# Geglu's x @ w_gate as four 32-row tiles of TensorE side by side, with x and the weights laid out by token block, and the output projection moved to the end

## The chip, the cores and the metric

The kernel runs on one core of a Trainium2 chip. The metric is device time in microseconds (us) of one execution; smaller is better. The profile of an execution is taken by the hardware profiler. Its engines are called PE (TensorE: matrix products), PEld (TensorE's weight loads, which are instructions of their own), DVE (VectorE), ACT (ScalarE), POOL (GpSimd) and SP (SyncE, which here issues every DMA, in the order of its queue). Matrix products write to PSUM, which has eight banks of 512 float32 columns; DVE and ACT read the results from there.

## The reference, cut to what matters

The output is a gated mix of an attention block and a geglu block over the same x (2048 tokens of width 448). The hidden width F is 1792, and there are 16 heads of 28.

```python
def _A_ref(x, wqkv, wo):            # attention, H = 16, Dh = 28
    q, k, v = split(x @ wqkv)
    p = softmax(q @ k.T * Dh ** -0.5)
    return merge_heads(p @ v) @ wo  # the output projection

def _B_ref(x, w_gate, w_up, w_down):
    return (_gelu(x @ w_gate) * (x @ w_up)) @ w_down

g = _sigmoid((x * gate_w).sum(-1, keepdims=True))
return g * _A_ref(x, wqkv, wo) + (1 - g) * _B_ref(x, w_gate, w_up, w_down)
```

Everything is float32. The kernel takes a float32 product as three products of a faster format (float32r): each operand is split exactly into hi + lo, and hi·hi + lo·hi + hi·lo is summed.

## The kernel before, in words

There are three stages. In the first, q, k, v and the gate's logits are made (tiles `pqk`, `pv`). In the second, attention runs head by head: score tiles `sc`, exp on ACT into `pt`, and values `po`, which are four products of 32 output columns each that stand side by side on TensorE. While ACT works on exp, TensorE takes `x @ w_up` in between, one product after the other, for all 14 tiles of 128 hidden columns (`pu`); it also takes `x @ w_gate` for the hidden tiles 0, 1 and 2 (NB = 3). The results (`u`) go to DRAM (`ud`) and are read back in the third stage.

The third stage is geglu, and the change is there. The hidden width is worked through in 7 chunks of FC = 2 tiles f of 128 columns, in the order (2, 3, 1, 4, 0, 5, 6), so it begins with the tiles 4 and 5. The tokens come in NTB = 4 blocks tb of 512. For each chunk and each block, `hidden(f, tb)` makes the gate product `pg`: 11 products of 128 rows of the contraction by 128 hidden columns by 512 tokens (the 448 rows are three tiles of 128 and one of 64, whose hi and lo parts share a tile; this is the list PAIRS). It needs no new x, since X with its hi and lo parts has been in SBUF since the first stage. For f < 3 `pg` is read from DRAM instead (`gs`). Then ACT applies gelu (L389), DVE multiplies by u (L390), ACT copies the hi part (L391) and DVE subtracts for the lo part (L392): the tile `hl2`. After a chunk's block, `down` takes the product with w_down for the block before it: 4 token tiles of 128, 6 products of 448 columns each into `pd`, and DVE adds each into `acc` (L407, L409). `load_f` fetches the weights of the next hidden tile in time: `load_half` (one DMA of 256 KB, hi on ACT L236, lo on DVE L232) and w_down (`draw`, `w`).

The output projection of attention is done in the middle of that stage: `load_wo` in chunk number 1, and in the chunks 2 and 3 `load_o` and `project` for each token block, 44 products of 448 columns that DVE adds into `acc` too. The last chunk's `down` adds `acc` into `y` and writes it out (L412, L413).

Matrix products keep the program's order (`mm`, L47). All other instructions are ordered by a scheduler when the kernel is built, so the order on SP, ACT and DVE is not quite that of the source. A tile that is allocated again waits until the readers of the older tile in its buffer are done; `bufs` says how many buffers a name has. The softmax division of a head (`finish`, L273 to L290) goes through DRAM in four steps on SP's queue: `dend`, `r`, `rdend`, `rb`, and then the result `od`; each step waits for the one before it.

Of the kernel before, what the change touches and what calls it, by code (L numbers as in the profile page):

```python
# [11 lines left out]
OP = mybir.AluOpType  # L12
# [30 lines left out]
def gated_mix(ctx: ExitStack, tc: tile.TileContext, xT, wqk, wvg, wg, wu, wd, wo, sel, ident, out):  # L43
# [18 lines left out]
    vp = attn.enter_context(tc.tile_pool(name="vp", bufs=1))  # L62
# [8 lines left out]
    with ExitStack() as ph:  # L71
# [74 lines left out]
        # |q.k| <= (sum of q's squared maxima + sum of k's) / 2, by head  # L146
# [28 lines left out]
        # g = 1 / (1 + exp(-t))  # L175
# [47 lines left out]
    gp = ctx.enter_context(tc.tile_pool(name="gp", bufs=1, side="right"))  # L223
# [15 lines left out]
    with ExitStack() as ph:  # L239
# [52 lines left out]
        def up():  # L292
            # x @ w_up, a product at a time
# [63 lines left out]
    with ExitStack() as ph:  # L357
        ap = ph.enter_context(tc.tile_pool(name="ap", bufs=1, reuse_waits="tile"))
        acc = ap.tile([P, NT, D], F32, name="acc")
        hp = ph.enter_context(tc.tile_pool(name="hp", bufs=2, reuse_waits="tile"))  # L360
        tp = ph.enter_context(tc.tile_pool(name="tp", bufs=3, reuse_waits="tile"))
        wpo = ph.enter_context(tc.tile_pool(name="wpo", bufs=1, reuse_waits="tile"))
        psg = ph.enter_context(tc.tile_pool(name="psg", bufs=3, space=PSUM, reuse_waits="tile"))
        psd = ph.enter_context(tc.tile_pool(name="psd", bufs=5, space=PSUM, reuse_waits="tile"))
        WD = {}

        def load_f(f):
# [3 lines left out]
            w = gp.tile([P, 2, D], F32R, name="w", bufs=3)  # L371
# [5 lines left out]
        def hidden(f, tb, hl):  # L377
            s = slice(tb * TB, (tb + 1) * TB)
            u = tp.tile([P, TB], F32, name="u")
            nc.sync.dma_start(out=u, in_=ud[f, :, s])  # L380
            g = tp.tile([P, TB], F32, name="g")
            if f < NB:
                pg = tp.tile([P, TB], F32, name="gs")
                nc.sync.dma_start(out=pg, in_=ud[NF + f, :, s])
            else:
                pg = psg.tile([P, TB], F32, name="pg")
                for i, (x, w) in enumerate(PAIRS):
                    mm(pg, halves["g", f][:, w], X[:, x, s], i == 0, i == len(PAIRS) - 1)
# [63 lines left out]
        for n in range(NF // FC):  # L452
            for tb in range(NTB):
                hls = []
                for k in range(n * FC, (n + 1) * FC):
                    if tb == 0 and k + 1 < NF:
                        load_f(order[k + 1])
# [48 lines left out]
```

## Time and profile before

| | |
|---|---|
| time, median of 2 runs | 1068.47 us (1068.43 to 1068.51) |
| span of the profiled execution (first to last instruction) | 1068.0 us |
| PE busy | 1054.2 us (99%), 5664 matrix products |
| ACT, DVE, POOL busy | 616.8, 320.2 and 41.5 us |
| geglu stage on PE | 777.5 to 1063.7 us of the span |
| DMA | 115.85 MB, 108 GB/s over the span |

In the page's groups, a row gives the line, the engine, the operation, out<-in by the program's names, the shapes (for PE rows contraction*output columns comes first) and the count; then the busy time of the group, the mean duration of one in ns, and the idle time of the engine just ahead of them with what ended it. Matrix products overlap in the pipeline, so that a group's busy time divided by its count, not the mean duration, says how long one keeps PE. Busy times, chains and timelines are in us from the start of the span.

### The profile page before, as it was taken

To read this page: it belongs to the slowest core of one execution; us is meant where nothing else is said; L and a number is where in the kernel's file an instruction comes from. 1 tells how busy PE (TensorE), PEld (TensorE's weight loads), DVE (VectorE), ACT (ScalarE), POOL (GpSimd) and SP (SyncE) were. 2 spreads that over 40 slices of the span, in tenths; PEclk is the share of its full clock that TensorE was granted. 3 is DMA by queue.
4 is the path that set the end of the run, shared out by engine and by line. 5 is a ranking of instruction groups with operands and counts; after the bars stand their busy time and mean duration, and the time that the engine had idled before them with its cause. 6 is when DMAs were issued, how large, how long until landed. Compare 5 with 4: busy or idle time off the path is not lost.

```text
span 1068.0 us, 14546 instructions
## 1 busy us (share of the span) xinstructions
PE 1054.2 (99%) x5664; PEld 732.2 (69%) x5664; DVE 320.2 (30%) x519; ACT 616.8 (58%) x732; POOL 41.5 (4%) x32
## 2 busy tenths in 40 slices
PE   7999999999999999999999999999999999999998
PEld 5789756556556556556556566565588888888887
DVE  5561111111111111110110110110156656577555
ACT  6322478778777777777777787787643332233321
POOL 5300000000000000000000000000001011100000
PEclk9999999999999999999999999999999999999999
DMA  8875122332332332342332332331164323342233
GB/s 267 291 258 145 57 75 73 120 103 73 102 103 74 98 107 73 94 112 73 94 112 73 93 111 73 94 102 41 64 191 142 99 86 91 95 148 67 63 87 115
DMA packets 58907, 115.85 MB, mean 108 GB/s; under 512 B 12784, under 2 KB 18160, under 8 KB 55216
## 3 DMA queue, kind: packets, MB, share of 16 engines
q1 hardware_dynamic: 58832, 114.85, 35.8%
q8 instruction: 47, 0.77, 0.3%
q14 instruction: 28, 0.23, 0.1%
HBM read 74.44 MB, written 40.37 MB: 108 GB/s over the span
## 4 chain that ended last, share of the span: by engine, by line
PE 88%; DVE 0%; issue 0%; DVEq 0%
PE sc L47 23%; PE po L47 21%; PE pd L47 16%; PE pu L47 16%; PE pg L47 11%; DVE u L307 0%; DVE y L412 0%; DVE gate L178 0%; DVE gate L177 0%; DVE gate L179 0%; DVEq L307 0%
## 5 line engine op out<-in xcount | busy, mean ns | idle before, releaser
L261 ACT ACTIVATE pt<-sc 128x1024 f32<-128x1024 f32 x512 | 482.4, 1026 | 164.6 <-PE sc L47 163.9
L47 PE MATMUL sc<-Q,K 114*128 114x512 f32 x1024 | 317.9, 402 | 1.3 <-issue 1.3
L47 PEld LDWEIGHTS sc<-Q,K 114*128 114x128 f32 x1024 | 188.8, 189 | 94.3 <-issue 54.5
L47 PE MATMUL pu<-X,half 128*128 128x512 f32 x748 | 237.8, 397 | 0.4 <-DVE u L307 0.3
L47 PE MATMUL po<-pt,V 128*32 128x512 f32 x2048 | 233.0, 595 | 0.0
L307 DVE COPY u<-pu 128x512 f32<-128x512 f32 x68 | 47.0, 691 | 491.6 <-PE pu L47 484.7
L47 PEld LDWEIGHTS pu<-X,half 128*128 128x128 f32 x748 | 141.0, 189 | 35.9 <-issue 1.4
L47 PEld LDWEIGHTS po<-pt,V 128*32 128x32 f32 x2048 | 60.0, 109 | 137.8 <-issue 132.2
L47 PE MATMUL pd<-w,hl 128*128 128x448 f32 x672 | 140.9, 366 | 0.0
L47 PEld LDWEIGHTS pd<-w,hl 128*128 128x128 f32 x672 | 126.2, 188 | 12.2
L47 PE MATMUL pg<-X,half 128*128 128x512 f32 x484 | 116.6, 395 | 0.0
L47 PEld LDWEIGHTS pg<-X,half 128*128 128x128 f32 x484 | 90.7, 187 | 20.9
L47 PE MATMUL pqk<-X,WQK 128*128 128x512 f32 x308 | 75.0, 404 | 7.7 <-ACT X L104 6.0
L47 PEld LDWEIGHTS pqk<-X,WQK 128*128 128x128 f32 x308 | 58.6, 192 | 23.7 <-ACT X L104 6.9
L389 ACT ACTIVATE g<-pg 128x512 f32<-128x512 f32 x44 | 26.2, 595 | 78.7 <-PE pg L47 78.6
L390 DVE TENSOR_TENSOR g<-g,u 128x512 f32<-128x512 f32 x56 | 46.0, 830 | 55.0 <-ACT g L389 55.0
L391 ACT ACTIVATE hl<-g 128x512 fp32r<-128x512 f32 x56 | 35.2, 630 | 42.4 <-DVE g L390 36.6
L409 DVE SCALAR_TENSOR_TENSOR acc<-pd,gate,acc 128x448 f32<-128x448 f32 x80 | 53.0, 679 | 6.8 <-PE pd L47 6.8
L437 POOL TENSOR_TENSOR ohl<-oraw,ohl 128x1536 fp32r<-128x1536 f32 x4 | 14.0, 3511 | 752.0 <-DMA u<-ud 749.2
L392 DVE TENSOR_TENSOR hl<-g,hl 128x512 fp32r<-128x512 f32 x56 | 38.3, 687 | 10.6 <-ACT hl L391 8.7
L47 PE MATMUL pd<-WO,ohl 128*128 128x448 f32 x176 | 37.0, 368 | 0.0
L47 PE MATMUL pv<-WV,X 128*128 128x450 f32 x176 | 36.4, 366 | 0.0
(60 smaller groups left out, 325.1 us busy)
## 6 DMA issues: line engine op xcount, KB each, us to landing
ud<-u SPq DMA_DIRECT2D x68, 256.0 KB
qkd<-hl SPq DMA_DIRECT2D x28, 512.0 KB
Q<-qkd SPq DMA_DIRECT2D x64, 224.0 KB
K<-qkd SPq DMA_DIRECT2D x64, 224.0 KB
u<-ud SPq DMA_DIRECT2D x56, 256.0 KB
raw<-in_xT SPq DMA_DIRECT2D x16, 256.0 KB
rb<-rdend SPq DMA_DIRECT2D x64, 64.0 KB
hraw<-in_wu SPq DMA_DIRECT2D x14, 256.0 KB
```

The source lines that it names most:

```text
L47: tc.keep_in_program_order(nc.tensor.matmul(o, lhsT, rhs, start=start, stop=stop))
L261: nc.scalar.activation(pt, sc, AF.Exp, scale=SCALE)
L307: nc.vector.tensor_copy(u, p)
L389: nc.scalar.activation(g, pg, AF.Gelu_apprx_tanh)
L390: nc.vector.tensor_tensor(g, g, u, OP.mult)
L391: nc.scalar.activation(hl[:, 0], g, AF.Copy)
L392: nc.vector.tensor_tensor(hl[:, 1], g, hl[:, 0].bitcast(F32), OP.subtract)
L409: nc.vector.scalar_tensor_tensor(acc[:, t], p, g1, acc[:, t], OP.mult, OP.add)
L437: nc.gpsimd.tensor_tensor(O[:, 4:7], o[:, 0:3], O[:, 0:3].bitcast(F32), OP.subtract)
```

## The change: what it does

The four token blocks of one hidden tile are now worked on together, each on 32 rows of TensorE. The contraction of 448 rows is cut into NCH = 14 chunks of 32. The new tile X2 holds x so that token block tb lies on the partitions 32·tb to 32·tb + 31 for all 14 chunks, as hi and lo. The weights `w2` of a hidden tile hold the same 14 chunks, copied onto all four groups of 32 partitions. For each chunk and each of the three hi/lo pairs, four products of 32 rows by 128 hidden columns by 512 tokens follow each other, one for each token block, into four PSUM banks: 14 × 3 × 4 = 168 products for a hidden tile, where there were 44.

With it come these changes:

- X and the pool `fw` are given up at the end of attention, and X2 is made from DRAM at the start of geglu (`load_x2`): 7 rounds, each with 8 DMAs of 64 KB into the one buffer `x2r`, a copy on ACT (hi) and a subtraction on DVE (lo).
- The weights of a hidden tile come by 16 DMAs into the one buffer `w2r`, in place of one DMA; the copy and the subtraction are 128x1792 in place of 128x512.
- The order of the chunks is (0, 1, ..., 6), so that geglu begins with the hidden tiles 0, 1 and 2, whose gate products come from DRAM.
- `hidden(f)` does all four blocks; two `down` of the chunk before follow each `hidden`. `psg` has 4 PSUM banks (3 before), `psd` 4 (5 before), `hl2` 10 buffers (4 before), `w` 5 (3 before), `u` 4 and `gs` 2 (3 before).
- The output projection with its loads comes last, after the last `down`; it adds `acc` into `y` and writes out. X2's memory is given up for it.

```diff
-ORDER = (2, 3, 1, 4, 0, 5, 6)   # chunks of the hidden width
+ORDER = (0, 1, 2, 3, 4, 5, 6)
+NCH = D // 32
...
-    X = keep.tile([P, 7, S], F32R, name="X")
-    fw = ctx.enter_context(tc.tile_pool(name="fw", bufs=2))
     attn = ctx.enter_context(ExitStack())
+    X = attn.enter_context(tc.tile_pool(name="xp", bufs=1)).tile([P, 7, S], F32R, name="X")
+    fw = attn.enter_context(tc.tile_pool(name="fw", bufs=2))
...
-        psg = ph.enter_context(tc.tile_pool(name="psg", bufs=3, space=PSUM, reuse_waits="tile"))
-        psd = ph.enter_context(tc.tile_pool(name="psd", bufs=5, space=PSUM, reuse_waits="tile"))
+        psg = ph.enter_context(tc.tile_pool(name="psg", bufs=4, space=PSUM, reuse_waits="tile"))
+        psd = ph.enter_context(tc.tile_pool(name="psd", bufs=4, space=PSUM, reuse_waits="tile"))
...
+        X2 = x2p.tile([P, 2, NCH, TB], F32R, name="X2")
+        def chunks(dst, src, q, g):
+            n = 4 if q < 2 else 3
+            nc.sync.dma_start(out=dst[32 * g:32 * g + 32, q:q + 4 * (n - 1) + 1:4], in_=src[32 * q:32 * q + 32, 0:n])
+        def load_x2():
+            for b in range(0, NCH, 2):
+                x2r = x2p.tile([P, 2, TB], F32, name="x2r", bufs=1)
+                for tb in range(NTB):
+                    for i in range(2):
+                        c = b + i
+                        nc.sync.dma_start(out=x2r[32 * tb:32 * tb + 32, i], in_=xT[tb, 32 * (c % 4):32 * (c % 4) + 32, c // 4])
+                nc.scalar.activation(X2[:, 0, b:b + 2], x2r, AF.Copy)
+                nc.vector.tensor_tensor(X2[:, 1, b:b + 2], x2r, X2[:, 0, b:b + 2].bitcast(F32), OP.subtract)
...
         def load_f(f):
             if f >= NB:
-                load_half(wg, f, "g", by_act)
+                w2r = w2p.tile([P, NCH, P], F32, name="w2r", bufs=1)
+                for q in range(4):
+                    for g in range(4):
+                        chunks(w2r, wg[f], q, g)
+                w2 = w2p.tile([P, 2, NCH, P], F32R, name="w2")
+                nc.scalar.activation(w2[:, 0], w2r, AF.Copy)
+                nc.vector.tensor_tensor(w2[:, 1], w2r, w2[:, 0].bitcast(F32), OP.subtract)
...
-                for i, (x, w) in enumerate(PAIRS):
-                    mm(pg, halves["g", f][:, w], X[:, x, s], i == 0, i == len(PAIRS) - 1)
+                steps = [(c, x, w) for c in range(NCH) for x, w in ((0, 0), (1, 0), (0, 1))]
+                for k, (c, x, w) in enumerate(steps):
+                    for tb in range(NTB):
+                        r = slice(32 * tb, 32 * tb + 32)
+                        mm(pgs[tb], WG2[f][r, w, c], X2[r, x, c], k == 0, k == len(steps) - 1)
...
+                made.append(hidden(order[k]))
+                for _ in range(2):
+                    if pend:
+                        down(*pend.pop(0))
+            pend = [(n, tb, [m[tb] for m in made]) for tb in range(NTB)]
+        xs.close()
...
+        load_wo()
+        for tb in range(NTB):
+            load_o(tb)
+        for p in pend:
+            down(*p)
+        for tb in range(NTB):
+            project(tb)
```

The order on PE where attention ends and geglu begins, before (names with numbers; `po` and `pu` are attention's last products, `pg` gate products, `pd` products with w_down):

```order
L47 MATMUL po_7755<-pt_7952,V_74 32x512 x2
L47 MATMUL pu_8005<-X_66,half_7610 128x512 x11
L47 MATMUL pg_8071<-X_66,half_8048 128x512 x11
L47 MATMUL pg_8101<-X_66,half_8058 128x512 x11
L47 MATMUL pg_8121<-X_66,half_8048 128x512 x11
L47 MATMUL pg_8141<-X_66,half_8058 128x512 x11
L47 MATMUL pd_8157<-w_8053,hl2_8067 128x448 x3
```

The same place on PE in the changed kernel:

```order
L48 MATMUL po_7755<-pt_7952,V_77 32x512 x2
L48 MATMUL pu_8005<-X_70,half_7610 128x512 x11
L48 MATMUL pd_8292<-w_8133,hl2_8159 128x448 x3
L48 MATMUL pd_8292<-w_8138,hl2_8204 128x448 x3
L48 MATMUL pd_8300<-w_8133,hl2_8159 128x448 x3
L48 MATMUL pd_8300<-w_8138,hl2_8204 128x448 x3
```

Ahead, four gate products of 11 stood at once behind attention's last product; now 48 products with w_down stand there, which need the finished `hl2` tiles of the hidden tiles 0 and 1.

A little further on PE in the changed kernel, the first gate product, of hidden tile 3, begins (`X2` and `w2` as in the diff, one `pg` for each token block):

```order
L48 MATMUL pd_8348<-w_8133,hl2_8165 128x448 x3
L48 MATMUL pd_8348<-w_8138,hl2_8210 128x448 x3
L48 MATMUL pg_8383<-X2_8054,w2_8244 128x512
L48 MATMUL pg_8386<-X2_8054,w2_8244 128x512
L48 MATMUL pg_8389<-X2_8054,w2_8244 128x512
L48 MATMUL pg_8392<-X2_8054,w2_8244 128x512
L48 MATMUL pg_8383<-X2_8054,w2_8244 128x512
```

The four token blocks now take turns product by product, where one block's 11 products stood together.

SP's queue from the last head's `finish` on, before:

```order
L277 DMA dend<-o 1x512 x4
L308 DMA ud<-u 128x512
L380 DMA u<-ud 128x512 x2
L280 DMA r<-dend 128x16
L421 DMA oraw<-in_wo 128x4x448
L282 DMA rdend<-r 128x16
L380 DMA u<-ud 128x512 x3
L285 DMA rb<-rdend 32x512 x4
L230 DMA hraw<-in_wg 128x512
L380 DMA u<-ud 128x512
```

SP's queue at the same place in the changed kernel (its second of seven rounds of `x2r` begins in the tenth row):

```order
L383 DMA x2r<-in_xT 32x512
L277 DMA dend<-o 1x512 x4
L308 DMA ud<-u 128x512
L383 DMA x2r<-in_xT 32x512 x2
L280 DMA r<-dend 128x16
L383 DMA x2r<-in_xT 32x512 x3
L282 DMA rdend<-r 128x16
L383 DMA x2r<-in_xT 32x512 x2
L402 DMA draw<-in_wd 128x448
L285 DMA rb<-rdend 32x512 x4
L413 DMA u<-ud 128x512
L383 DMA x2r<-in_xT 32x512 x3
```

The loads for x stand between the steps of `finish`, and the first load of u, with which geglu begins, has moved behind `rb`.

ACT's queue around one hidden tile's gelu, before (`g<-pg` and `g<-gs` are gelu, `hl` the hi copy, `half<-hraw` the gate weights' hi copy):

```order
L389 ACTIVATE g<-pg 128x512
L391 ACTIVATE hl_8516<-g 128x512
L389 ACTIVATE g<-pg 128x512
L236 ACTIVATE half<-hraw 128x512
L391 ACTIVATE hl_8568<-g 128x512
```

ACT's queue around the gelu of hidden tile 3 in the changed kernel (`w_8666<-w2r` is the hi copy of the gate weights of hidden tile 5):

```order
L430 ACTIVATE g<-pg 128x512 x3
L432 ACTIVATE hl_8562<-g 128x512
L432 ACTIVATE hl_8568<-g 128x512
L397 ACTIVATE w_8666<-w2r 128x1792
L430 ACTIVATE g<-pg 128x512
L432 ACTIVATE hl_8574<-g 128x512
```

The weights' copy for the hidden tile after next has moved ahead of the gelu of the fourth token block.

More of the change, by code (lines that the diff above doesn't have):

```diff
@@ L407, in down @@
                     nc.vector.tensor_scalar(acc[:, t], p, g1, None, OP.mult)
-                elif c < NF // FC - 1:
+                else:
                     nc.vector.scalar_tensor_tensor(acc[:, t], p, g1, acc[:, t], OP.mult, OP.add)
-                else:
-                    y = tp.tile([P, D], F32, name="y")
-                    nc.vector.scalar_tensor_tensor(y, p, g1, acc[:, t], OP.mult, OP.add)
-                    nc.sync.dma_start(out=out[0, t * P:(t + 1) * P], in_=y)
+        order = [f for c in ORDER for f in range(c * FC, (c + 1) * FC)]
+        load_f(order[0])
+        pend = []
+        for n in range(NF // FC):
+            made = []
+            for k in range(n * FC, (n + 1) * FC):
+                if k + 1 < NF:
+                    load_f(order[k + 1])
+                made.append(hidden(order[k]))
[4 more added lines that the diff above has]
+        xs.close()
+        wpo = ph.enter_context(tc.tile_pool(name="wpo", bufs=1, reuse_waits="tile"))
         WO = wpo.tile([P, 8, D], F32R, name="WO")
@@ L446, in project @@
                     mm(p, O[:, x, i * P:(i + 1) * P], WO[:, w], k == 0, k == len(PAIRS) - 1)
-                nc.vector.scalar_tensor_tensor(acc[:, t], p, gate[:, 1, t:t + 1], acc[:, t], OP.mult, OP.add)
-        order = [f for c in ORDER for f in range(c * FC, (c + 1) * FC)]
-        load_f(order[0])
-        pend = None
[L452 to L457, printed above, removed]
-                    hl = hp.tile([P, 2, TB], F32R, name="hl2", bufs=4)
-                    hidden(order[k], tb, hl)
-                    hls.append((order[k], hl))
-                if pend:
-                    down(*pend)
-                pend = n, tb, hls
-                if n == 1 and tb == 0:
-                    load_wo()
-                if n in (2, 3) and tb % 2 == 0:
-                    load_o((n - 2) * 2 + tb // 2)
-                if n in (2, 3) and tb % 2 == 1:
-                    project((n - 2) * 2 + tb // 2)
-        down(*pend)
+                y = tp.tile([P, D], F32, name="y")
+                nc.vector.scalar_tensor_tensor(y, p, gate[:, 1, t:t + 1], acc[:, t], OP.mult, OP.add)
+                nc.sync.dma_start(out=out[0, t * P:(t + 1) * P], in_=y)
+        load_wo()
+        for tb in range(NTB):
+            load_o(tb)
+        for p in pend:
+            down(*p)
+        for tb in range(NTB):
+            project(tb)
 def kernel(A_x, A_wqkv, A_wo, B_x, B_w_gate, B_w_up, B_w_down, gate_w):
```

52 lines of the change are left out of this document (32 added, 20 removed).

## Prediction

> **What bounds the kernel now.** I read the page's busy times first, then its chain of waits, then the chain in order of time through the geglu stage.
>
> ```profile
> span 1068.0 us, 14546 instructions
> PE 1054.2 (99%) x5664; PEld 732.2 (69%) x5664; DVE 320.2 (30%) x519; ACT 616.8 (58%) x732; POOL 41.5 (4%) x32
> PE 88%; DVE 0%; issue 0%; DVEq 0%
> ...
> 777.47 10.27 PE pg L47 x44
> 787.73 4.90 PE pd L47 x24
> ...
> 862.81 13.98 PE pd L47 x68
> ...
> 1053.91 9.81 PE pd L47 x48
> ```
>
> TensorE never pauses: the chain is made of matrix products, and in geglu one block follows the other from 777.5 to 1063.7 us. So the kernel's time is the sum of what its products keep PE for, and any wait of PE is added in full. What one product keeps PE for comes from these rows: a gate product 10.27/44 = 0.233 us, a `pd` product with w_down 4.90/24 = 0.204, one of the output projection (13.98 − 4.90)/44 = 0.206 (of the 68, 24 are w_down's). After the last product come 1068.0 − 1063.7 = 4.3 us for `y` and its write.
>
> **The gate products.** A hidden tile has 44 products now, 44 × 0.233 = 10.3 us. Afterwards it has 168 in 42 groups of four. If a group keeps PE no longer than one product does now, that is 42 × 0.233 = 9.8 us, half a microsecond less; over 11 hidden tiles 107.8 against 113.0, a gain of 5. This is all that the change can win, since the other products stay as many. No product on 32 rows is in this trace. The nearest are attention's values, four products on 32 output columns each; the timeline of PE and of its weight loads shows them:
>
> ```profile
> 768.31 2.83 PE L47 MATMUL pu<-X,half 128*128 128x512 f32 x11
> 771.06 3.64 PE L47 MATMUL po<-pt,V 128*32 128x512 f32 x32
> 774.63 2.83 PE L47 MATMUL pu<-X,half 128*128 128x512 f32 x11
> ...
> 772.38 0.13 PEld L47 LDWEIGHTS po<-pt,V 128*32 128x32 f32 x4 [0.30 <-issue]
> 772.81 0.13 PEld L47 LDWEIGHTS po<-pt,V 128*32 128x32 f32 x4 [0.30 <-issue]
> ...
> L47 PE MATMUL po<-pt,V 128*32 128x512 f32 x2048 | 233.0, 595 | 0.0
> L47 PEld LDWEIGHTS po<-pt,V 128*32 128x32 f32 x2048 | 60.0, 109 | 137.8 <-issue 132.2 <-DVE u L307 5.3 <-DMA Q<-qkd 0.4
> L47 PEld LDWEIGHTS pg<-X,half 128*128 128x128 f32 x484 | 90.7, 187 | 20.9
> L47 PE MATMUL pb<-sq,selt 128*16 128x1 f32 x14 | 0.5, 164 | 0.0
> ```
>
> Every 0.43 us four loads begin within 0.13 us, although one takes 0.109, and four products run in that time while one lasts 0.595. So four tiles do run side by side here, columns at least. I take 0.233 for a group of four, by this nearest row. From below the bound is 42 × 0.43/2 (`po`'s groups in halves, since their products are longer), 9.0 us, 8 us less in all. From above it is no overlap at all, 168 × 0.233. Changing from full products to tiles and back costs PE, by the first three rows, (2.75 − 11 × 0.233) + (3.57 − 8 × 0.43) = 0.3 us; 11 hidden tiles make 3.3.
>
> **The start of geglu.** Before, gate products stood there that needed nothing new (X lay in SBUF). Now PE first has 48 `pd` products, and behind these the gate product of hidden tile 3, which needs all of X2 and `w2`. X2's 7 rounds go through one buffer, and their 56 DMAs, 16 DMAs for `w2r` and 34 others stand in SP's single queue, between the steps of the last head's `finish`. The same steps before, in the timelines of SP, DVE and ACT, with the groups whose sizes lie around the new ones:
>
> ```profile
> 779.72 1.21 SPq L280 DMA_DIRECT2D r<-dend  x1
> 784.15 0.33 SPq L282 DMA_DIRECT2D rdend<-r  x1
> 786.92 1.82 SPq L285 DMA_DIRECT2D rb<-rdend  x4
> 793.87 1.64 SPq L289 DMA_DIRECT2D od<-o  x4
> 825.08 0.33 SPq L372 DMA_DIRECT2D draw<-in_wd  x1
> 827.48 0.58 ACT L373 ACTIVATE w<-draw 128x448 fp32r<-128x448 f32 x1 [1.51 <-DMA draw<-in_wd]
> ...
> L391 ACT ACTIVATE hl<-g 128x512 fp32r<-128x512 f32 x56 | 35.2, 630 | 42.4 <-DVE g L390 36.6 <-PE pd L47 5.7
> L433 ACT ACTIVATE ohl<-oraw 128x1536 fp32r<-128x1536 f32 x4 | 6.0, 1488 | 30.9 <-PE pd L47 20.6 <-issue 9.3 <-DMA oraw<-od 1.1
> L422 ACT ACTIVATE WO<-oraw 128x1792 fp32r<-128x1792 f32 x1 | 1.7, 1690 | 0.0
> L392 DVE TENSOR_TENSOR hl<-g,hl 128x512 fp32r<-128x512 f32 x56 | 38.3, 687 | 10.6 <-ACT hl L391 8.7
> L423 DVE TENSOR_TENSOR WO<-oraw,WO 128x1792 fp32r<-128x1792 f32 x1 | 2.0, 2027 | 0.9 <-ACT WO L422 0.9
> ```
>
> A DMA of 64 KB (`rb`) takes SP 1.82/4 = 0.45 us; from issue to use `draw` needed 827.48 − 825.08 = 2.4 us. For 1024 columns I estimate ACT at 1.06 us (between 0.63 and 1.49) and DVE at 1.22 (between 0.69 and 2.03). A round, from the first issue to the subtraction that frees `x2r`, is then 7 × 0.45 + 2.4 + 1.06 + 1.22 = 7.8 us. The first round's last two DMAs stand behind `rdend` (784.15), so its last issue is at 784.9 and it ends at 784.9 + 2.4 + 2.3 = 789.6. The second has `od`'s four issues in its middle and ends some 2 us later than a plain one, at 799.5. Five more bring 838.5; the other DMAs between them (2 to 3 us a round) fit into the 4.7 us in which SP waits anyway. Behind the last copy ACT has `w2`'s, 1.69 us, and DVE its subtraction, 2.03, so that the gate products begin at 840. At 0.33 us an issue and 1.5 us of landing a round is 6.1 us and the begin 828; with 10 us a round it is 853. In front of that PE can do just the 48 `pd` products, which wait for gelu of `gs` tiles that are loaded between the rounds: 9.8 us of work in 62.5. PE stands still for 53 us. What is late next is PE's clock:
>
> ```profile
> core 0: us, PE busy (x) PEld busy (x) DVE busy (x) ACT busy (x) POOL busy (x), PEclk, DMA share, GB/s
> 7.20:10.40 3.20, 3.14 (x7) 2.44 (x8) 3.10 (x5) 2.91 (x6) 1.14 (x1) 1.00 0.97 300
> 10.70:13.10 2.40, 2.40 (x12) 1.94 (x11) 1.49 (x4) 1.33 (x3) 0.00 (x0) 1.00 0.84 273
> ```
>
> After its first idle stretch PE did 7 products in 3.2 us, and 12 in 2.4 a little later; such a start costs 3.2 − 7 × 0.233 = 1.5 us.
>
> **The weights' 16 DMAs.** In the steady state they are hidden: 16 × 0.45 + 2.4 + 1.7 + 2.0 = 13 us, against a period of 9.8 + 48 × 0.204 = 19.6 us. Not so for the first ones. ACT has the copy of tile 5's weights ahead of the fourth gelu of tile 3, whose PSUM bank tile 4 needs. `w2r` for tile 4 can be issued after 841 and is split at 854, that for tile 5 lands at 864, and with 1.69 and 0.6 us the bank comes free at 866; PE is there at 840 + 1.5 + 9.8 + 9.8 + 0.3, about 862. So PE waits some 4 us (0 to 7), once. Without this late start there would be no wait.
>
> **Answered at nothing.** The groups of the gelu and the sums, and of the projection's split on POOL:
>
> ```profile
> L389 ACT ACTIVATE g<-pg 128x512 f32<-128x512 f32 x44 | 26.2, 595 | 78.7 <-PE pg L47 78.6
> L390 DVE TENSOR_TENSOR g<-g,u 128x512 f32<-128x512 f32 x56 | 46.0, 830 | 55.0 <-ACT g L389 55.0
> L409 DVE SCALAR_TENSOR_TENSOR acc<-pd,gate,acc 128x448 f32<-128x448 f32 x80 | 53.0, 679 | 6.8 <-PE pd L47 6.8
> L437 POOL TENSOR_TENSOR ohl<-oraw,ohl 128x1536 fp32r<-128x1536 f32 x4 | 14.0, 3511 | 752.0 <-DMA u<-ud 749.2
> ```
>
> Gelu, products and splits are as many as before, and ACT (4 × 0.6 + 4 × 0.63 + 1.7 + 0.6 = 7 us) and DVE (4 × 0.83 + 4 × 0.69 + 8 × 0.68 + 2.0 + 0.6 = 14 us) stay under 19.6 us a hidden tile. The hi copies of blocks 3 and 4 wait for `down` to give `hl2` back, behind the gelu that frees the bank; nobody needs them for 10 us. The projection's loads begin when the last gate product is done, 30 us of `pd` products ahead of `project`; a block's split on POOL, 3.5 us, is far shorter than its 9.1 us on PE. The tail stays 4.3 us.
>
> **The sum**, in the profiled execution: 840 + 1.5 + 107.8 + 4 + (672 − 48) × 0.204 = 127.4 + 176 × 0.206 = 36.3 + 3.3 + 4.3 = 1124.6. The median of the runs, 1068.47, lies 0.5 above the span, so 1125. With 828 to 853 for the start and 9.0 to 10.3 us for a hidden tile this case has a range of its own, 1105 to 1143.
>
> **The rivals.**
>
> *The weight loads bind.* A load of 128 columns takes 187 ns, one of 32 takes 109: 0.81 ns a column, 104 for 128. If the loads of four row tiles follow each other (or a tile's load has to wait for its own product, 233 + 187), a group takes 420 ns, 17.6 us a hidden tile, 11 × 7.8 = 86 more, less the 4 of wait: 1207. For it: four loads of 32 columns (4 × 26 ns) would fit one after the other into `po`'s 430 ns, so these rows don't exclude it. Against it: four loads overlap there, and a gate product's load overlaps the product ahead on the same rows. The Trainium skill, "TensorE: Matmul & The Clock Gate", section "The mechanism", says that a weight load overlaps a running product only when their row groups differ; taken literally this rule gives the 420, and the trace does not bear it out, since a gate product of today would take 233 + 187 by it as well, and takes 233. I give it 0.18.
>
> *They stagger.* The 14 `pb` products of one column follow each other at (0.5 − 0.164)/13 = 26 ns. If each of a group's four is held up by that, a group takes 233 + 3 × 26 = 311 ns, 13.1 us a hidden tile, 36 more and no wait: 1157. `po`'s spacing within 0.13 us speaks against it. Chance 0.14. The same page's section "Measured speedup vs the span model" gives 3.07 for four row tiles, not 4; the group would take 304 ns, and the sum by it would be 1154.
>
> *Not side by side at all* (the change doesn't do what it says): 168 × 0.233 = 39.2 us, 11 × 29.4 = 323 more: 1444. Chance 0.06.
>
> *The start is hidden, and it is not slower.* The first DMA of x2r waits for a late exp, not for attention's end, and stands ahead of `dend` in the queue. If all of X2 came under attention's products, the 53 us, the cold start and the wait would go: 1067. It is no slower by 2% from a start at 804 on, which asks for rounds of 2.4 us, the landing alone. Chance 0.04.
>
> **How the numbers follow.** The forecast has 0.58. About 2% can be told from no change here. From 1105 to 1210 lie nearly all of the forecast's case, the stagger and most of the binding loads: 0.8 and a little. Slower by over 2% are all cases but the last, and for what I don't see I leave 0.08: faster 0.03, same 0.05, slower 0.92.
>
> **What would show it.** In the profile after: PE idle for about 50 us between 777 and 840 with only 48 `pd` products, released by ACT or DVE work on `x2r` and `w2r`; rounds of 8 DMAs at distances near 8 us on SP; 168 `pg` products in 9.8 us (17.6 would be the loads, 13 the stagger); one short wait of PE for gelu before tile 4; the last 37 us a row of projection products without gaps. Wrong would make it: X2 ready before 805, or a group of four that is not near 0.233.

## The result

The changed kernel takes 1173.99 us (median of 2 runs, 1172.89 to 1175.1) against 1068.47: ratio 1.0986, 95% interval 1.0965 to 1.1006. It is slower by 105 us. The prediction had 1125, a loss of 56. The time lies inside its range of 1105 to 1210, but above the 1105 to 1143 that the forecast's own case was given.

The page of the profile after, with the lines that answer to those of before (after the busy times come the busy tenths of PE and its granted clock in 40 slices of 29 us, then the chain by engine and the groups of the gate products):

```profile
span 1171.1 us, 17653 instructions
PE 1070.4 (91%) x7028; PEld 742.8 (63%) x7028; DVE 336.6 (29%) x526; ACT 631.2 (54%) x739; POOL 40.5 (3%) x32
...
PE   7999999999999999999999999953368988989998
...
PEclk9999999999999999999999999985688989999999
...
PE 66%; SPq 9%; DVE 6%; DMA 5%; issue 2%; ACT 2%; DVEq 0%; ACTq 0%
...
L48 PE MATMUL pg<-X,w 32*128 32x512 f32 x1848 | 111.2, 394 | 18.4 <-ACT w L397 17.6
L48 PEld LDWEIGHTS pg<-X,w 32*128 32x128 f32 x1848 | 93.3, 187 | 35.1 <-ACT w L397 17.9
```

Attention is as before. Where geglu begins PE has a hole (5336), and behind it eights between the nines; the clock is down in the hole and at the first two of the eights behind it. PE is on the chain for 66% of the span, not 88, and SP's queue has 9%. The 1848 gate products keep PE busy for 111.2 us, a little less than the 484 did before (116.6 by the same row of that page): the tiles do run side by side.

The timeline of PE through the start of geglu (start, duration, then in brackets the idle time before and what ended it):

```profile
774.03 2.79 PE L48 MATMUL pu<-X,half 128*128 128x512 f32 x11
799.46 1.92 PE L48 MATMUL pd<-w,hl 128*128 128x448 f32 x3 [22.64 <-ACT hl L432]
811.28 7.45 PE L48 MATMUL pd<-w,hl 128*128 128x448 f32 x24 [9.90 <-ACT hl L432]
...
843.19 1.23 PE L48 MATMUL pg<-X,w 32*128 32x512 f32 x8 [17.57 <-ACT w L397]
845.25 11.61 PE L48 MATMUL pg<-X,w 32*128 32x512 f32 x160 [0.83 <-DVE w L398]
856.79 5.13 PE L48 MATMUL pd<-w,hl 128*128 128x448 f32 x24
867.24 4.21 PE L48 MATMUL pd<-w,hl 128*128 128x448 f32 x12 [5.32 <-DVE acc L450]
877.17 4.36 PE L48 MATMUL pd<-w,hl 128*128 128x448 f32 x12 [5.72 <-DVE acc L450]
```

The first gate product begins at 843.2 (forecast 840), with 52.1 us of idle time up to there and 0.8 right behind (forecast 53). But the waits go on behind it. The timeline of all engines over one tile pair of the steady state shows one of them from its cause to its end:

```profile
974.83 9.84 PE L48 MATMUL pg<-X,w 32*128 32x512 f32 x168
974.97 2.01 DVE L398 TENSOR_TENSOR w<-w2r,w 128x1792 fp32r<-128x1792 f32 x1
...
977.04 9.91 SPq L375 DMA_DIRECT2D w2r<-in_wg  x16
...
984.60 5.21 PE L48 MATMUL pd<-w,hl 128*128 128x448 f32 x24
987.05 4.26 SPq L402 DMA_DIRECT2D draw<-in_wd  x2
989.71 0.58 ACT L403 ACTIVATE w<-draw 128x448 fp32r<-128x448 f32 x1 [14.80 <-DMA draw<-in_wd]
990.19 1.55 ACT L430 ACTIVATE g<-pg 128x512 f32<-128x512 f32 x3
...
990.86 1.89 DVE L431 TENSOR_TENSOR g<-g,u 128x512 f32<-128x512 f32 x3
...
992.71 1.68 ACT L397 ACTIVATE w<-w2r 128x1792 fp32r<-128x1792 f32 x1
...
993.87 1.27 DVE L452 SCALAR_TENSOR_TENSOR acc<-pd,gate,acc 128x448 f32<-128x448 f32 x2
...
994.60 7.75 PE L48 MATMUL pd<-w,hl 128*128 128x448 f32 x24 [4.79 <-DVE acc L452]
...
1001.75 2.02 DVE L398 TENSOR_TENSOR w<-w2r,w 128x1792 fp32r<-128x1792 f32 x1
```

It is a ring: each step below waits for the one ahead of it, and the last one holds up the first again. DVE's split gives `w2r` back at 977.0. SP issues the 16 DMAs for the next weights, 9.9 us or 0.62 each (the forecast had 0.45). Only then do the two `draw` loads come, and the first lands at 989.7. ACT has the copy of `draw` ahead of the gelus in its program and stands for 14.8 us, although the gate products were done at 984.6. So gelu is late, DVE has `g*u` ahead of the sums and so the sums are late, and PE, out of `pd` banks, waits 4.79 us. Its next 24 products then take 7.75 us instead of the 5.21 of the block before. ACT's copy of the next weights (992.71) follows the gelus, and DVE's split, which frees `w2r` again, stands behind seven such sums, the last of which wait for PE's slow products: it comes 26.8 us after the last one, where a tile has 19.6 us of work. The `draw` loads come in pairs, so it is so in every second tile; the pass before, without them, took 20.5 us (954.48 to 974.97).

The difference of the spans, 1171.1 − 1068.0 = 103.1 us, is then nearly all accounted for (PE's gaps of over 0.1 us, from the same timeline over the whole stage, in sums): 52.9 at the start, 33.3 in later waits (11.0 of them in the first tile pair, 3.5 at the projection's beginning, the rest in every second tile), and 16.2 more busy time (1070.4 − 1054.2), since products at a lowered clock take longer (the 672 `pd` products with w_down have 158.5 us on the page, where they had 140.9).

### The profile page after: what moved, and what is told of

Same layout as the page of the kernel before. It is cut to its first block, busy times and chain, and to the rows that moved or that the text cites. A ratio compares the mean times of both kernels' runs of the same rounds, so it can differ in the third digit from the quotient of the medians.

```text
span 1171.1 us, 17653 instructions
## 1 busy us (share of the span) xinstructions
PE 1070.4 (91%) x7028; PEld 742.8 (63%) x7028; DVE 336.6 (29%) x526; ACT 631.2 (54%) x739; POOL 40.5 (3%) x32
## 4 chain that ended last, share of the span: by engine, by line
PE 66%; SPq 9%; DVE 6%; DMA 5%; issue 2%; ACT 2%; DVEq 0%; ACTq 0%
PE sc L48 21%; PE po L48 20%; PE pu L48 15%; PE pd L48 8%; SPq L375 7%; PE pg L48 3%; SPq L383 1%; DVE w L398 1%; DVE g L431 1%; DVE acc L452 1%; DMA gs<-ud 1%; DMA u<-ud 1%; DMA w2r<-in_wg 1%; DMA draw<-in_wd 1%; ACT w L397 1%
## 5 line engine op out<-in xcount | busy, mean ns | idle before, releaser
L48 PE MATMUL pd<-w,hl 128*128 128x448 f32 x672 | 158.5, 395 | 68.0 <-ACT hl L432 33.9
L48 PEld LDWEIGHTS pd<-w,hl 128*128 128x128 f32 x672 | 135.2, 205 | 91.0 <-ACT hl L432 35.3
L48 PE MATMUL pg<-X,w 32*128 32x512 f32 x1848 | 111.2, 394 | 18.4 <-ACT w L397 17.6
L48 PEld LDWEIGHTS pg<-X,w 32*128 32x128 f32 x1848 | 93.3, 187 | 35.1 <-ACT w L397 17.9
L430 ACT ACTIVATE g<-pg 128x512 f32<-128x512 f32 x44 | 23.6, 591 | 85.4 <-PE pg L48 84.2
L452 DVE SCALAR_TENSOR_TENSOR acc<-pd,gate,acc 128x448 f32<-128x448 f32 x96 | 61.7, 677 | 7.7 <-PE pd L48 7.7
L431 DVE TENSOR_TENSOR g<-g,u 128x512 f32<-128x512 f32 x56 | 36.6, 686 | 67.7 <-ACT g L430 67.7
L403 ACT ACTIVATE w<-draw 128x448 fp32r<-128x448 f32 x14 | 8.0, 574 | 73.3 <-DMA draw<-in_wd 58.9
L489 POOL CAST ohl<-oraw 64x512 fp32r<-64x512 f32 x4 | 2.4, 606 | 1085.4 <-PE pd L48 1078.0
```

The costliest lines, as they stand in the source:

```text
L48: tc.keep_in_program_order(nc.tensor.matmul(o, lhsT, rhs, start=start, stop=stop))
L430: nc.scalar.activation(g, pgs[tb], AF.Gelu_apprx_tanh)
L431: nc.vector.tensor_tensor(g, g, us[tb], OP.mult)
L452: nc.vector.scalar_tensor_tensor(acc[:, t], p, g1, acc[:, t], OP.mult, OP.add)
```

## The experiments

All times are medians beside runs of the kernel before on the same chip (1068.4 to 1069.6 us). Every kernel here computes the whole result; where a layout differs, the host orders a copy of the weights or of x.

```
kernel                    us       ratio to before [95%]     first gate product  PE idle after 765
changed kernel            1174.0   1.0986 [1.0965, 1.1006]   843.2               86.3
weights_4_dmas            1135.1   1.0622 [1.0566, 1.0678]   835.0               55.8
x_1_dma                   1156.0   1.0818 [1.0786, 1.0849]   824.9               70.0
w2r_2_buffers             1141.2   1.0679 [1.0645, 1.0713]   844.4               62.5
draw_2_buffers            1152.0   1.0774 [1.0747, 1.0800]   842.9               73.0
both_layouts              1114.8   1.0430 [1.0411, 1.0448]   823.3               41.4
both_layouts_2_buffers    1116.3   1.0423 [1.0397, 1.0449]   824.6               42.1
both_layouts_old_order    1129.8   1.0562 [1.0545, 1.0580]   808.9               53.0
old_order_draw_2          1121.9   1.0494 [1.0474, 1.0514]   807.2               47.2
old_order                 1162.5   1.0872 [1.0845, 1.0898]   811.8               75.7
tail_no_pool              1172.7   1.0965 [1.0943, 1.0987]   843.2               83.0
no_tiles                  1092.4   1.0223 [1.0193, 1.0252]   808.8               18.8
```

### Is it the weights' DMAs?

```
-                for q in range(4):
-                    for g in range(4):
-                        chunks(w2r, wg[f], q, g)
+                for g in range(4):
+                    nc.sync.dma_start(out=w2r[32 * g:32 * g + 32], in_=wg2[f])
```

> The changed kernel, but the gate weights lie in DRAM in the order in which w2r wants them (the host reorders them), so that a hidden tile needs 4 DMAs of 32 long rows instead of 16 of short ones. Theory (a ring through SP's queue: 16 issues of 0.6 us, behind them the loads of w_down, whose copy on ACT stands ahead of gelu, behind gelu the DVE work that frees the pd banks): the waits of PE after the start, 33 us, and the half-speed products after them go, and the products of one hidden tile follow the last one's at about 20 us everywhere: 1120 to 1135 us. Rival 1 (four pd banks instead of five, and DVE's own load, keep PE waiting): the waits stay, 1160 or more. Rival 2 (the 32-row products cost more than they seem, by switching and by the clock): 1160 or more.

1135.06 us (1132.87 to 1137.24), 39 less, of which 8 come from the first gate product (835.0). The timelines of SP and PE in its steady state:

```profile
990.31 1.72 SPq L394 DMA_DIRECT2D w2r<-in_wg  x4
992.13 6.30 SPq L401 DMA_DIRECT2D draw<-in_wd  x2
```

```profile
968.73 9.84 PE L48 MATMUL pg<-X,w 32*128 32x512 f32 x168
978.49 9.99 PE L48 MATMUL pd<-w,hl 128*128 128x448 f32 x48
988.41 9.84 PE L48 MATMUL pg<-X,w 32*128 32x512 f32 x168
```

With 1.7 us of issues in place of 9.9, PE runs a tile every 19.7 us without a gap. The same bytes come in, in fewer DMAs of longer rows; this run alone can't tell SP's time per DMA from a faster transfer. The next two kernels leave the DMAs as they are.

### The same ring, cut at another place

In `w2r_2_buffers` the number of DMAs stays, and SP need not wait for DVE's split (`y` moves to another pool to make room). In `draw_2_buffers` the second `draw` load need not wait for the first one's split.

```
-                w2r = w2p.tile([P, NCH, P], F32, name="w2r", bufs=1)
+                w2r = w2p.tile([P, NCH, P], F32, name="w2r", bufs=2)
-                y = tp.tile([P, D], F32, name="y")
+                y = wpo.tile([P, D], F32, name="y", bufs=3)
```

> The changed kernel, but w2r has two buffers (the output tile y has moved to the projection's pool to make room). SP issues as many DMAs as before, but a tile's weight loads no longer wait for the subtraction of the tile before. Theory (ring): the ring is cut at that wait and the loads of w_down come early enough: 1125 to 1145 us. If SP's issue time by itself is the bound (16 x 0.6 + 4 u + w_down, 13 to 18 us in a period of 20): little changes at first, 1155 or more. Rival (pd banks, DVE): no change, 1165 or more.

```
-            draw = gp.tile([P, D], F32, name="draw")
+            draw = gp.tile([P, D], F32, name="draw", bufs=2)
```

> As the changed kernel, but draw has two buffers: the second of a pair of draw loads no longer waits on SP until ACT and DVE have split the first. Theory (the ring goes from DVE's split of w through 16 issues of w2r, the draw loads behind them, ACT's copy and the gelus behind that): the ring loses the wait of the second draw load, some 3.6 of the 4.3 us that the pair takes on SP, in each of five or six late tiles; with the cold clock behind each wait 18 to 25 us less in all, 1148 to 1160, gate distances nearer to 23 than to 27 us in every second tile. Rival (only the 16 w2r issues matter, draw is a bystander that has time): the same as the changed kernel, 1168 to 1176.

`w2r_2_buffers`: 1141.15 us (1140.35 to 1141.95); the start is as long as ever (844.4), and from the second one on the gate blocks come every 19.7 us, though 16 DMAs are still issued for each. `draw_2_buffers`: 1152.0 (1149.12 to 1154.84); SP's timeline:

```profile
966.09 9.85 SPq L375 DMA_DIRECT2D w2r<-in_wg  x16
976.03 0.85 SPq L402 DMA_DIRECT2D draw<-in_wd  x2
976.98 3.85 SPq L413 DMA_DIRECT2D u<-ud  x4
986.65 9.98 SPq L375 DMA_DIRECT2D w2r<-in_wg  x16
```

The pair takes 0.85 us instead of 4.26, the gate blocks come some 20.5 us apart, and of the 33.3 us of late waits 19.3 are left (73.0 − 53.7 at the start), all but 4 of them in the first tile pair and at the projection. So `draw` is no bystander, and the 16 issues alone don't make the wait: it takes the whole ring, and a cut at any of three places (the issues, the first buffer, the second) takes most of the waits in the later tiles away (18.8 us; 0, 0 and 4 are left). The waits in the first tile pair are another matter: of their 11.0 us, 8.3 are left with the weights' layout, 8.3 with two `w2r` buffers and 11.8 with two for `draw`.

### Is the start a separate thing?

```
-                for tb in range(NTB):
-                    for i in range(2):
-                        c = b + i
-                        nc.sync.dma_start(out=x2r[32 * tb:32 * tb + 32, i], in_=xT[tb, 32 * (c % 4):32 * (c % 4) + 32, c // 4])
+                nc.sync.dma_start(out=x2r, in_=x2[:, b:b + 2])
```

> The changed kernel, but x lies in DRAM also in the order of X2, so that each of the 7 rounds is one DMA instead of 8. Theory (the start is bound by the rounds through the one buffer x2r): a round is 0.45 + 2.4 + 1.06 + 1.22 = 5.1 us instead of 7.8, the first gate product begins 14 to 18 us sooner than 843, and all else stays: 1155 to 1160 us. Rival (the start is bound by what stands between the rounds, the finish chain and the 16 weight DMAs): the start moves by less than 6 us, 1168 or more.

1155.98 us (1155.52 to 1156.43), and the first gate product 18.3 us sooner, 18.0 of which reach the end. The late waits stay. Both layouts together:

> Both layouts of the host at once: one DMA a round for X2, four a tile for the weights. Theory (the loss is two separate things, the start and the ring of SP, ACT and DVE): their gains add, since they lie in different stretches. Weights' layout alone gave 1135.1 and its first gate product at 835.0; X2's alone moved the first one by 18.3 us (843.2 to 824.9). So the first gate product at about 817 and the time 1117, between 1112 and 1122, with gate blocks every 19.7 us behind the first two tiles. Rival (one common cause: whatever makes the start shorter only lets PE wait longer behind it, for the loads that SP has not done): the first gate product comes sooner but the distances grow, and the time stays at 1127 or above.

1114.79 us (1114.07 to 1117.55). 38.9 + 18.0 = 56.9 were to come off 1174.0, which makes 1117.1: the times add, and the rival falls. The start did not come as the theory had it, though: the first gate product is at 823.3, not 817. Shorter waits behind it (5.4 us in the first tile pair, 8.3 with the weights' layout alone) and less busy time at a higher clock (0.980 over the span, 0.972 there) make up for that. Of the loss 45 us are left, most of it at the start. PE there:

```profile
787.63 1.84 PE L48 MATMUL pd<-w,hl 128*128 128x448 f32 x3 [11.30 <-ACT hl L428]
810.20 12.59 PE L48 MATMUL pd<-w,hl 128*128 128x448 f32 x45 [20.73 <-ACT hl L428]
823.31 0.74 PE L48 MATMUL pg<-X,w 32*128 32x512 f32 x8 [0.52 <-ACT w L393]
825.50 9.40 PE L48 MATMUL pg<-X,w 32*128 32x512 f32 x160 [1.45 <-DVE w L394]
```

Of these 34 us of idle time, 32 end with `hl`, the gelu's output of a tile that was loaded from DRAM, and not with X2 or `w2`. But the loads of those tiles (`gs`, `u`) stand on SP between X2's rounds, each of which waits for the one buffer `x2r`. So that buffer was doubled next.

### Two buffers for x2r, and the order of the chunks

(`y` moves to the other pool as in `w2r_2_buffers`, here and in the next two kernels.)

```
-                x2r = x2p.tile([P, 2, TB], F32, name="x2r", bufs=1)
+                x2r = x2p.tile([P, 2, TB], F32, name="x2r", bufs=2)
```

> As both_layouts, and x2r has two buffers, so that a round's load does not wait for the split of the round before it. Theory: a round is then set by its slowest engine (about 1.2 us on DVE) and the queue instead of the whole loop of issue, landing, ACT and DVE; seven rounds fit behind the last exp, and the start is bound by the last head's normalization (done near 800) and the first gelus of the tiles in DRAM: the first gate product at 805 to 812, the time 1103 to 1112. What is left against before is then the order, which cost 24 us by itself, less 5 for the tiles, plus the loads of the first weights. Rival (the landing and SP's queue bind the rounds, not the buffer): as both_layouts, 1115 or above.

1116.28 us (1111.76 to 1118.42): no gain. The theory missed with its time and with the first gate product (824.6); the rival's number came, but not for its reason, since X2 was ready early, as DVE's last split of it (L382) shows, beside PE's timeline:

```profile
799.93 1.23 DVE L382 TENSOR_TENSOR X<-x2r,X 128x1024 fp32r<-128x1024 f32 x1 [2.69 <-ACT X L381]
```

```profile
803.75 1.84 PE L48 MATMUL pd<-w,hl 128*128 128x448 f32 x3 [26.86 <-ACT hl L428]
812.33 12.17 PE L48 MATMUL pd<-w,hl 128*128 128x448 f32 x45 [6.75 <-ACT hl L428]
824.58 0.74 PE L48 MATMUL pg<-X,w 32*128 32x512 f32 x8
```

X2 is complete at 801, but PE's program has the 48 `pd` products first. They wait for gelus of the tiles from DRAM, whose loads now stand behind X2's in the queue. The next kernel adds the old order, which begins with tiles whose gate products are computed:

```
-ORDER = (0, 1, 2, 3, 4, 5, 6)
+ORDER = (2, 3, 1, 4, 0, 5, 6)
```

> As both_layouts_2_buffers, with the chunks in the order of the kernel before (2, 3, 1, 4, 0, 5, 6), so that geglu begins with a tile whose gate products are computed and the tiles from DRAM come fifth. Theory (there X2 was ready near 801 and PE still began its gate products at 824.6, because its program puts 48 pd products ahead of them, which wait for the gelus of tiles loaded from DRAM behind X2): the first gate product begins at 800 to 806, PE has work from there on, and the sum is 803 + 11 x 9.8 + 672 x 0.204 + 36.3 + 1.5 + 3.3 + 4.3 = 1093, with small waits 1092 to 1100. Rival (the order makes no difference, since the loads of X2 and of the first weights set the start in both): 1112 or above.

1129.83 us (1128.6 to 1132.97): slower by 13.6 than with the new order, where the theory had 16 to 24 less. The rival's time came, but not its reason: the order does make a difference, the gate products begin 16 us sooner, at 808.9, and then PE waits again:

```profile
808.88 1.23 PE L48 MATMUL pg<-X,w 32*128 32x512 f32 x8 [30.88 <-ACT w L393]
810.95 10.91 PE L48 MATMUL pg<-X,w 32*128 32x512 f32 x160 [0.84 <-DVE w L394]
831.28 1.76 PE L48 MATMUL pg<-X,w 32*128 32x512 f32 x3 [9.42 <-ACT g L426]
835.94 12.42 PE L48 MATMUL pg<-X,w 32*128 32x512 f32 x165 [2.90 <-ACT g L426]
```

With no sums to do yet, one gate block follows the other through four PSUM banks, and each has to wait for the gelus. On ACT a copy of `draw` stood ahead of the first gelu, so `draw` got two buffers here, too:

> As both_layouts_old_order, and draw has two buffers. That kernel began its gate products at 808.9 as foreseen, but gave 1129.8 instead of 1092 to 1100: PE then waited 9.42, 2.90, 0.53 and 3.19 us for gelu. Theory (the first gelu, on ACT at 829.3, stood behind a copy of draw at 828.74, whose load stood on SP from 823.9 to 830.3 because the only draw buffer had to be split first; with no sums between the first gate blocks PE has nothing else): with two buffers the wait of 9.42 falls to 2 to 4 us and the time by 6 to 12 us, to 1117 to 1124. Rival (the first gelu is late for another reason: the copies of w2r, or its table load of 1.28 us): 1127 or above, with a wait still near 9 us.

1121.92 us (1121.33 to 1124.52): in place of 9.42 us PE waits 0.66 there, and 8 us of time are gone, as the theory had it. The waits of a run of gate blocks stay: the next one has grown from 2.90 to 5.56, the last is 3.19 again. And the new order, even with one `draw` buffer, remains better by 6 us (1116.3).

The order alone, put back in the changed kernel:

> The changed kernel with only the order of the chunks put back (2, 3, 1, 4, 0, 5, 6). Theory (with X2 in 56 DMAs X2 is late whatever the order, and the 48 pd products were the only work in front of it): the first gate product stays between 832 and 843, the 9.8 us of pd products move behind it, so PE's idle stretch grows to 55 to 65 us; the ring of the weights stays: 1170 to 1185. Rival (the new order is what costs, as in both_layouts_old_order): 1140 to 1155.

1162.49 us (1161.15 to 1163.83), 11.5 less, between the two expectations. The first gate product comes at 811.8, 31 us sooner, which I had thought impossible: the gate products go chunk by chunk, so PE can begin on X2's first rounds, and then waits for the splits of the last two (8.3 us in all). That the first tile "needs all of X2" before it can begin was wrong. In the changed kernel it didn't show: what PE waited for last, at 843, was `w2`, whose last two DMAs stand on SP behind X2's last round.

### What the rest of the change costs without tiles

In `no_tiles` the gate products are those of the kernel before: X stays in SBUF through geglu, no X2, no `w2r`. The order of the chunks and the projection's place at the end are those of the change.

```
-                for k, (c, x, w) in enumerate(steps):
-                    for tb in range(NTB):
-                        r = slice(32 * tb, 32 * tb + 32)
-                        mm(pgs[tb], WG2[f][r, w, c], X2[r, x, c], k == 0, k == len(steps) - 1)
+                for tb in range(NTB):
+                    for i, (x, w) in enumerate(PAIRS):
+                        mm(pgs[tb], halves["g", f][:, w], X[:, x, tb * TB:(tb + 1) * TB], i == 0, i == len(PAIRS) - 1)
```

> The gate products as they were before the change (X kept in SBUF, 44 products of 128 rows, one weight DMA), in the changed kernel's order: chunks 0 to 6, four blocks of a hidden tile together, projection last. Theory: what is lost comes from building X2 and w2. PE waits only for the first gelu of tiles read from DRAM, 8 to 20 us, and then runs without waits: 1076 to 1092 us. Rival (the order and the late projection cost it): 1120 or more.

1092.39 us (1091.91 to 1092.88), at the upper end of what was expected. What the change does besides the tiles (the order, four blocks together, the buffers, the late projection) costs 24 us by itself, and PE shows where (timeline at geglu's start):

```profile
787.60 1.92 PE L48 MATMUL pd<-w,hl 128*128 128x448 f32 x3 [8.80 <-ACT hl L402]
797.19 11.75 PE L48 MATMUL pd<-w,hl 128*128 128x448 f32 x45 [7.67 <-ACT hl L402]
808.78 10.19 PE L48 MATMUL pg<-X,half 128*128 128x512 f32 x44
```

16.5 us are waits for the tiles from DRAM, with which the new order begins, and 2.3 a wait at the projection; the remaining 3 us of the spans' difference (1090.1 − 1068.0) are busy time, with a clock of 0.988 over the span. So the tiles with their two layouts cost the other 82 us (1174.0 − 1092.4).

### The slow split at the projection

DVE's split of WO took 2.03 us before. In the changed kernel (timelines of DVE and of POOL):

```profile
1107.41 5.25 DVE L478 TENSOR_TENSOR WO<-oraw,WO 128x1792 fp32r<-128x1792 f32 x1
```

```profile
1107.27 3.51 POOL L492 TENSOR_TENSOR ohl<-oraw,ohl 128x1536 fp32r<-128x1536 f32 x1 [0.20 <-ACT ohl L488]
```

```
-            nc.gpsimd.tensor_tensor(O[:, 4:7], o[:, 0:3], O[:, 0:3].bitcast(F32), OP.subtract)
+            nc.vector.tensor_tensor(O[:, 4:7], o[:, 0:3], O[:, 0:3].bitcast(F32), OP.subtract)
```

> As the changed kernel, but the projection's lo split of a block of od (128x1536) runs on DVE instead of POOL. Theory (DVE's split of WO took 5.25 us instead of 2.03 because POOL's split ran beside it): it takes 2.0 to 2.1 us here, PE's waits of 2.00 and 1.53 us at the projection's beginning go or shrink to under 1.5 in all, and the time is 1169 to 1174 (2 to 4 us less at most). Rival (the split is slow for another reason, such as the DMA traffic at that moment): it still takes above 3 us.

The split takes 2.02 us, and the waits of 2.00 and 1.53 us at the projection shrink to 0.65; DVE does POOL's work in half its time:

```profile
1110.29 2.02 DVE L478 TENSOR_TENSOR WO<-oraw,WO 128x1792 fp32r<-128x1792 f32 x1
1113.65 1.76 DVE L492 TENSOR_TENSOR ohl<-oraw,ohl 128x1536 fp32r<-128x1536 f32 x1
```

In the time, 1172.72 (1172.51 to 1172.93) against 1172.89 to 1175.1, a gain of this size can't be told.

No version beat the kernel before. What is left in the best one, 45 us, lies mostly at the start (34 us of waits in `both_layouts`), where nothing is ready for PE: with the new order it waits for the gelus of the tiles from DRAM, with the old one for the first weights and then for the gelus of its own gate blocks. To load X2 under attention's products X and X2 would have to lie in SBUF together; that wasn't tried.

## Why the prediction was right, and where it was wrong

**The start: right in its mechanism, and the number in part by luck.** 843.2 for 840, idle time 52.9 for 53, and `x_1_dma` showed that the issues of the rounds make a third of it. But two errors partly cancel in the 840. DVE had done the second round at 796.2, not 799.5, and the five after it took 46.7 us, not 39. The fourth alone took 14.0 us in place of 7.8: ACT was done with it at 812.4, and DVE's split began at 817.5, behind three sums that waited for PE. This is already the fault of the ring, an order on a queue that the forecast left out. The cold start behind it was sized too small: the first tile takes 13.6 us from its first product to the first `pd` (856.79 − 843.19), 3.8 more than a warm one with 0.8 of it a wait, where 1.5 was forecast. The granted clock was 0.50 there up to 848 and full from 851; the row from which the forecast took its 1.5 us has a granted clock of 1.00, and so was no measure of a cold start.

**The group of four, right.** 168 products in 9.77 us (974.83 to 984.60), 0.233 a group with the change of tiles included. Neither rival on the products shows: 311 or 420 ns would have made 13 or 17.6 us. A tile gains the forecast's half microsecond (9.77 for 10.27). The Trainium skill, "TensorE: Matmul & The Clock Gate", section "The mechanism", has in its list that a weight load overlaps only products on other row groups, though the text ahead of the list also lets a load into a background buffer run ahead. Here loads of 187 ns on the same four row groups as the products ahead cost nothing, so the trace does not bear out the list's "only". The same page's "Measured speedup vs the span model" has 3.07 for four row tiles; blocks of 42 groups back to back reach 4.0 (168 × 0.233/9.77), if a product by itself is put at the 0.233 us of a 128-row one.

**The step that failed** is "The weights' 16 DMAs", with its "In the steady state they are hidden: 16 × 0.45 + 2.4 + 1.7 + 2.0 = 13 us, against a period of 9.8 + 48 × 0.204 = 19.6 us". The sum was of one transfer that runs by itself. An issue took 0.62 us, not 0.45, which alone would have made 16 us and still have fitted. What it left out is what stands behind each part in a queue: `draw` behind the issues on SP, the gelus behind `draw`'s copy on ACT, the sums behind `g*u` on DVE, and `w2r`'s own split behind seven sums. In every second tile the ring takes 26.8 us. Where the forecast had no wait at all, the runs showed 18.8 us in later tiles, and the lowered clock after the waits of 4 to 5 us on top. The three cuts of the ring, 39 us by the layout (8 of it at the start), 33 by a buffer for `w2r`, 22 by one for `draw`, and the 19.7 us a tile without it, bear this out.

The wait that the same paragraph did forecast, "4 us (0 to 7), once", came by nearly the path that it names, in ACT's timeline:

```profile
873.61 1.70 ACT L397 ACTIVATE w<-w2r 128x1792 fp32r<-128x1792 f32 x1 [8.17 <-DMA w2r<-in_wg]
875.22 0.58 ACT L430 ACTIVATE g<-pg 128x512 f32<-128x512 f32 x1
```

The copy of tile 5's weights stands ahead of tile 3's fourth gelu, but at 873.6 and not at 864, and PE stopped for want of a `pd` bank, behind DVE's sums, before it came to the gate products. Together with the wait behind the copy of tile 4's weights it made 11.0 us. As 8.3 of these are left when the ring is cut, most of this wait is not the ring's. That it comes of the late start, as the forecast said, fits the 5.4 us of `both_layouts`, but was not tested by itself.

With the ring cut (1135) the time lies inside the forecast's own range. That 1174 still lies below 1210 is luck: the range reached so far for the stagger and the binding loads, and neither came.

**Answered at nothing**, half wrong. DVE and ACT do stay under 19.6 us of work a tile, but that is a statement on their sums, and it was their order that bound. The copy of `draw` has its 0.6 us in ACT's sum, and no place in ACT's order. The projection's split on POOL was costed as hidden beside PE; it held up DVE, and PE lost 3.5 us. The row for it was on the page: L390's mean of 830 ns, beside 687 for an operation of the same shape.

**What the runs corrected besides.** The change of order was given no price of its own. Without the tiles PE waits 16.5 us for it; in the changed kernel the old order is better by 11.5 us, with both layouts the new one by 6 to 14. So it has no price apart from the rest. The projection at the end runs without gaps, as forecast.

## What to carry to other kernels

A load that is "hidden" because its own steps are shorter than the period has still to be followed through every in-order queue that it shares: what stands behind its issues, behind its conversion, and what its buffer's release stands behind. When a new layout is gathered with many small DMAs, count the issues on the one queue first; a copy in the right order in DRAM, or one more buffer, was worth four to eight times the 5 us that the faster products could win. And when PE is the bound, a wait of some 4 us or more costs more than its length here, since the products behind it run at a lowered clock.

## What the runs showed of the hardware that was not expected

*DVE and POOL.* The split of WO on DVE began at 1107.41 beside POOL's, which ran until 1110.78; it ended at 1112.66, 1.9 us after POOL, and it takes 2.02 alone. By these times it did not share with POOL, it stood still until POOL had ended. The Trainium skill, "SBUF — State Buffer", section "Who interferes with whom", describes such an exclusive lock; the trace agrees (5.25 us beside POOL, 2.02 without). The kernel before shows the same four times: of its 56 products `g*u` on DVE (L390) four ran beside a split of POOL's. These took 3.68, 2.15, 2.43 and 2.43 us in place of 0.69, and each ended 0.5 to 0.6 us behind POOL, which makes up all of the raised mean. Sums that read `pd` from PSUM (L503) took 0.68 us beside POOL's splits, as they do elsewhere.

*The clock after short waits.* A wait of 5 us is enough to slow PE: 24 products behind 4.79 us took 7.75 us, 24 without a wait 5.21. A wait of 2.00 us at the projection left the clock as it was. The granted clock over the ring's stretch, behind the 4.79 us and behind the 2.00 us, is the third number from the end of each row:

```profile
843.00:1100.00 257.00, 226.13 (x2339) 193.27 (x2340) 131.84 (x193) 72.22 (x115) 0.00 (x0) 0.93 0.35 98
994.60:1002.35 7.75, 7.75 (x28) 6.71 (x28) 6.00 (x10) 1.43 (x3) 0.00 (x0) 0.63 0.27 78
1113.31:1116.00 2.69, 2.69 (x12) 2.23 (x13) 2.66 (x5) 0.00 (x0) 0.00 (x0) 1.00 0.70 225
```

*Issue time.* In the steady state the 16 DMAs of 64 and 48 KB with rows of 512 bytes took SP 0.62 us each; four of 32 long rows, which bring the same weights, took 0.43 each (1.72/4).
